# Decode attention over a 65,536-key cache: K turned by VectorE in 32x32 blocks of 32-bit words, a whole chunk's scores in one PSUM bank, four buffers in place of five

## The chip, the cores and the metric

The kernel runs on one core of a Trainium2 chip. The metric is device time in microseconds (us) of one execution. The kernel before takes 1289.4 us (median of 3 runs, 1289.29 to 1289.5). The span in a profile is about 1.7 us shorter than the device time of the same execution. Engines: PE is TensorE's matmul, PEld its weight load, DVE is VectorE, ACT is ScalarE, POOL is GpSimd, SP issues the large loads. "DMA share" is the mean busy share of the core's 16 DMA engines; the "granted clock" is the share of full speed at which PE was allowed to run.

## The reference

One query token, 16 query heads on 8 K/V heads, 65,536 keys of 256 numbers, bfloat16. A small token mixer (branch B) and a gate are mixed in. Cut to what matters:

```python
Hq, Hkv, Sk, Dh = 16, 8, 65536, 256              # x: [1, 1, 448]
q = (x @ wq).reshape(B, Sq, Hq, Dh).transpose(0, 2, 1, 3)
k = jnp.repeat(k_cache, 2, axis=1)               # k_cache, v_cache: [1, 8, 65536, 256]
v = jnp.repeat(v_cache, 2, axis=1)
p = softmax(einsum("bhqd,bhkd->bhqk", q, k) * Dh ** -0.5)
a = einsum("bhqk,bhkd->bhqd", p, v).reshape(B, Sq, Hq * Dh) @ wo
out = g * a + (1 - g) * b                        # b: token mixer, g: gate
```

K and V are 537 MB together and are read once. Everything else is small.

## The kernel before

Each K or V item is a chunk of 8192 keys, 4 MB, in one of five ring buffers. A chunk is worked in four steps of 2048 keys. K comes with keys on the partitions, and this kernel's score matmuls read it with the 256 dimensions there. So PE transposes K (read as 32-bit words, two bfloat16 each) into PSUM, DVE copies that to SBUF, and PE multiplies with the queries in four column strips.

```python
NB = 64; CHUNK = 128 * NB; SB = 16; STEPS = NB // SB; RING = 5; LAG = 4
...
def transposes(n, half):                    # called twice per step
    kn = ring[2 * (n // STEPS) % RING][:].bitcast(FP32).rearrange("p (j k) -> p j k", k=128)
    tp = tps[half]
    j0 = (n % STEPS) * SB + 8 * half
    for jj in range(8):
        nc.tensor.transpose(tp[:, 128 * jj:128 * jj + 128], kn[:, j0 + jj, :], ident[:])
    nc.vector.tensor_copy(
        out=kT[n % 2][:, 8 * DH * half:8 * DH * (half + 1)], in_=tp[:].bitcast(BF16)
    )

def scores(n):
    ...
    for c in range(2):
        for a in range(4):
            nc.tensor.matmul(
                sc[n % 2][32 * a:32 * a + 32, :], lhsT=qT[:, c, g].rearrange("p r x -> p (r x)"),
                rhs=kv[:, :, 32 * a:32 * a + 32, c], start=(c == 0), stop=(c == 1),
                tile_position=(0, 32 * a),
            )
    nc.scalar.activation(out=p_t[n % 2][:], in_=sc[n % 2][:], func=ACT.Exp, scale=scale, accum_out=...)

def p_transpose(n):
    nc.vector.transpose(out=pT_t[n % NPT][:], in_=p_t[n % 2][:])
...
for n in range(n_steps + LAG):
    if n < n_steps:
        transposes(n, 0)
    if 0 <= n - 1 < n_steps:
        scores(n - 1)
    if n < n_steps:
        transposes(n, 1)
    if 0 <= n - 1 < n_steps:
        p_transpose(n - 1)
    ...
    m = n - LAG                              # PV runs four steps behind
    ...                                      # p_v(m): 8 matmuls of 512 columns; then the loads
```

The softmax here doesn't subtract the row's maximum and nothing guards it: scores larger than these inputs give would overflow.

## Time and profile before

| | before |
|---|---|
| device time, median | 1289.4 us |
| span of the profile | 1287.6 us |
| busy PE, DVE, ACT | 74%, 62%, 15% |
| DMA share, 40 to 1240 us | 1.00 |
| last K/V packet ends | 1279.9 us |

Busy time by stretches of the kernel before. The columns are the stretch, its length, busy us of PE, PEld, DVE, ACT and POOL, the granted PE clock, the DMA share and GB/s.

```profile
40.00:640.00 600.00, 447.45 (x3912) 278.66 (x3912) 371.22 (x395) 98.09 (x268) 70.10 (x72) 0.84 1.00 430
640.00:1240.00 600.00, 450.89 (x3966) 281.07 (x3963) 371.03 (x391) 83.98 (x245) 2.31 (x3) 0.85 1.00 429
1266.00:1270.00 4.00, 4.00 (x43) 2.70 (x40) 3.82 (x4) 1.32 (x4) 0.00 (x0) 1.00 0.86 351
1270.00:1274.00 4.00, 4.00 (x45) 2.21 (x43) 3.63 (x5) 0.74 (x3) 0.00 (x0) 1.00 0.58 240
1274.00:1278.00 4.00, 3.22 (x39) 1.96 (x40) 3.82 (x5) 0.69 (x2) 0.00 (x0) 1.00 0.52 209
1278.00:1282.00 4.00, 2.75 (x42) 1.02 (x42) 2.04 (x6) 0.69 (x2) 0.00 (x0) 1.00 0.08 28
```

The mid-kernel is DMA-bound. At the end the DMA does not stop at once. From about 1270 us it runs at a share near 0.5 for some 9 us.

Groups of instructions of the kernel before (line, engine, operation, out<-in, shapes, count | busy us, mean ns | idle time before it and what ended it). K is copied from PSUM four times in this form, 620 us of DVE in all.

```profile
L316 DVE COPY kT_141<-tps_74 128x2048 bf16<-128x2048 bf16 x128 | 154.8, 1209 | 350.5 <-PE tps_74 L315 350.5
L315 PE MATMUL tps_74<-ident,ring_69 128*128 128x128 f32 x416 | 68.7, 318 | 66.6 <-DMA ring_69<-in_A_k_cache_dram 66.5
L325 PE MATMUL sc_77<-kT_142,qT 128*32 128x512 bf16 x1024 | 105.0, 495 | 1.2 <-DVE kT_142 L316 1.2
```

The end of the kernel before, from the timeline (start us, duration us, engine and line, operation, out<-in, count, [idle before <-releaser]):

```profile
1277.92 0.62 PE L325 MATMUL sc_77<-kT_142,qT 128*32 128x512 bf16 x8 [0.78 <-DVE kT_142 L316]
1280.89 0.60 PE L347 MATMUL pv<-ring_71,pT_148 128*4 128x512 bf16 x8
1281.55 0.75 DVE L364 TENSOR_SCALAR pvs<-pv,rden 128x512 f32<-128x512 f32 x1 [0.62 <-PE pv L347]
1285.26 0.32 SPq L432 DMA_DIRECT2D out_dram<-res  x1
```

### The profile page before, as it was taken

What the parts mean: (1) busy time and instruction counts of PE and PEld (TensorE: products, weight loads), DVE (VectorE), ACT (ScalarE), POOL (GpSimd) and SP (SyncE); (2) the same over time, 40 slices, a digit from 0 to 9 for tenths busy, and PEclk for the clock granted to TensorE, in tenths of its full rate; (3) what the DMA queues carried; (4) which work ended last, traced back from release to release, by engine and by line L of the source; (5) the groups of instructions that cost most, each with busy time, mean ns of one, the idle gap of its engine ahead of it and who ended that gap; (6) DMA issues with size and microseconds to landing.
All of it is one profiled execution on the core that took longest, in us unless ns stands there. A gap on an engine that the chain in (4) does not pass through costs nothing.

```text
span 1287.6 us, 19500 instructions
## 1 busy us (share of the span) xinstructions
PE 952.5 (74%) x8454; PEld 595.9 (46%) x8454; DVE 792.6 (62%) x859; ACT 193.2 (15%) x543; POOL 80.2 (6%) x101
## 2 busy tenths in 40 slices
PE   4586777876877767778768677696786876877878
PEld 3354444544544444445445444454454544544544
DVE  3565755756666557566566575674665755656657
ACT  0111111211111111111111111111111111111111
POOL 2110111100111001110000000000000000000000
PEclk9887888888888788788888897887887888889889
DMA  9999999999999999999999999999999999999995
GB/s 392 431 430 433 427 432 425 429 432 429 433 425 433 429 431 428 429 430 429 432 429 426 433 430 430 430 430 427 435 427 433 425 430 431 430 430 418 436 421 241
DMA packets 21196, 545.49 MB, mean 424 GB/s; under 512 B 2675, under 2 KB 2806, under 8 KB 3958
## 3 DMA queue, kind: packets, MB, share of 16 engines
q1 hardware_dynamic: 19730, 540.55, 98.0%
q0 software_dynamic: 1376, 3.69, 0.8%
q8 instruction: 66, 1.08, 0.3%
q14 instruction: 20, 0.16, 0.0%
q10 hardware_dynamic: 4, 0.00, 0.0%
HBM read 544.22 MB, written 0.00 MB: 423 GB/s over the span
## 4 chain that ended last, share of the span: by engine, by line
DMA 62%; PE 37%; DVE 1%; issue 0%; ACT 0%; SPq 0%; ACTq 0%; DVEq 0%
DMA ring_73<-in_A_k_cache_dram 15%; PE tps_74 L315 12%; DMA ring_69<-in_A_k_cache_dram 12%; DMA ring_72<-in_A_k_cache_dram 12%; PE tps_75 L315 12%; DMA ring_71<-in_A_k_cache_dram 12%; DMA ring_70<-in_A_k_cache_dram 11%; PE pv L347 6%; PE sc_77 L325 4%; PE sc_76 L325 3%; DMA ring_73<-in_A_wq_dram 1%; PE misc L292 0%; PE misc L247 0%; DVE kT_142 L316 0%; PE misc L357 0%
## 5 line engine op out<-in xcount | busy, mean ns | idle before, releaser
L316 DVE COPY kT_141<-tps_74 128x2048 bf16<-128x2048 bf16 x128 | 154.8, 1209 | 350.5 <-PE tps_74 L315 350.5
L316 DVE COPY kT_141<-tps_75 128x2048 bf16<-128x2048 bf16 x128 | 156.4, 1222 | 95.2 <-PE tps_75 L315 94.8
L331 ACT ACTIVATE p_144<-sc_77 128x512 bf16<-128x512 f32 x128 | 76.4, 597 | 710.0 <-PE sc_77 L325 710.0
L316 DVE COPY kT_142<-tps_75 128x2048 bf16<-128x2048 bf16 x128 | 156.7, 1224 | 25.2 <-PE tps_75 L315 24.6
L316 DVE COPY kT_142<-tps_74 128x2048 bf16<-128x2048 bf16 x128 | 152.7, 1193 | 7.8 <-PE tps_74 L315 7.3
L331 ACT ACTIVATE p_143<-sc_76 128x512 bf16<-128x512 f32 x128 | 76.4, 597 | 368.8 <-PE sc_76 L325 368.8
L315 PE MATMUL tps_74<-ident,ring_69 128*128 128x128 f32 x416 | 68.7, 318 | 66.6 <-DMA ring_69<-in_A_k_cache_dram 66.5
L315 PE MATMUL tps_74<-ident,ring_71 128*128 128x128 f32 x416 | 68.8, 319 | 65.5 <-DMA ring_71<-in_A_k_cache_dram 65.5
L315 PE MATMUL tps_74<-ident,ring_70 128*128 128x128 f32 x416 | 66.0, 310 | 63.5 <-DMA ring_70<-in_A_k_cache_dram 63.5
L315 PE MATMUL tps_74<-ident,ring_73 128*128 128x128 f32 x416 | 67.0, 313 | 58.5 <-DMA ring_73<-in_A_k_cache_dram 58.0
L315 PE MATMUL tps_74<-ident,ring_72 128*128 128x128 f32 x384 | 62.3, 315 | 63.8 <-DMA ring_72<-in_A_k_cache_dram 63.8
L325 PE MATMUL sc_77<-kT_142,qT 128*32 128x512 bf16 x1024 | 105.0, 495 | 1.2 <-DVE kT_142 L316 1.2
L315 PEld LDWEIGHTS tps_74<-ident,ring_71 128*128 128x128 f32 x416 | 54.6, 163 | 91.5 <-issue 89.4
L315 PEld LDWEIGHTS tps_74<-ident,ring_69 128*128 128x128 f32 x416 | 54.8, 163 | 89.6 <-issue 88.0
L315 PEld LDWEIGHTS tps_74<-ident,ring_70 128*128 128x128 f32 x416 | 52.3, 158 | 86.6 <-issue 84.9
L315 PEld LDWEIGHTS tps_74<-ident,ring_73 128*128 128x128 f32 x416 | 53.1, 160 | 82.4 <-issue 77.6
L315 PEld LDWEIGHTS tps_74<-ident,ring_72 128*128 128x128 f32 x384 | 49.3, 161 | 85.3 <-issue 83.6
L325 PE MATMUL sc_76<-kT_141,qT 128*32 128x512 bf16 x1024 | 79.3, 385 | 0.2
L315 PE MATMUL tps_75<-ident,ring_69 128*128 128x128 f32 x416 | 67.8, 316 | 0.0
L315 PE MATMUL tps_75<-ident,ring_71 128*128 128x128 f32 x416 | 66.7, 312 | 0.0
L315 PEld LDWEIGHTS tps_75<-ident,ring_69 128*128 128x128 f32 x416 | 53.8, 161 | 26.9 <-issue 26.9
L315 PEld LDWEIGHTS tps_75<-ident,ring_71 128*128 128x128 f32 x416 | 52.8, 159 | 27.6 <-issue 27.6
(133 smaller groups left out, 976.5 us busy)
## 6 DMA issues: line engine op xcount, KB each, us to landing
ring_69<-in_A_k_cache_dram SPq DMA_DIRECT2D x13, 4096.0 KB, 25.1
ring_70<-in_A_v_cache_dram SPq DMA_DIRECT2D x13, 4096.0 KB, 34.5
ring_71<-in_A_k_cache_dram SPq DMA_DIRECT2D x13, 4096.0 KB, 24.8
ring_72<-in_A_v_cache_dram SPq DMA_DIRECT2D x13, 4096.0 KB, 34.2
ring_73<-in_A_k_cache_dram SPq DMA_DIRECT2D x13, 4096.0 KB, 24.5
ring_69<-in_A_v_cache_dram SPq DMA_DIRECT2D x13, 4096.0 KB, 33.9
ring_70<-in_A_k_cache_dram SPq DMA_DIRECT2D x12, 4096.0 KB, 24.2
ring_71<-in_A_v_cache_dram SPq DMA_DIRECT2D x12, 4096.0 KB, 33.6
```

What stands on the lines that cost most here:

```text
L315: nc.tensor.transpose(tp[:, 128 * jj:128 * jj + 128], kn[:, j0 + jj, :], ident[:])
L316: nc.vector.tensor_copy(out=kT[n % 2][:, 8 * DH * half:8 * DH * (half + 1)], in_=tp[:].bitcast(BF16))
L325: nc.tensor.matmul(sc[n % 2][32 * a:32 * a + 32, :], lhsT=qT[:, c, g].rearrange("p r x -> p (r x)"), rhs=kv[:, :, 32 * a:32 * a + 32, c], ...
L331: nc.scalar.activation(out=p_t[n % 2][:], in_=sc[n % 2][:], func=ACT.Exp, scale=scale, accum_out=den[g % 2][:, n % steps_g:n % steps_g + 1],)
L347: nc.tensor.matmul(pv[32 * a:32 * a + 4, :], lhsT=pT[:, i, :, 0], rhs=vt[:, j * DH:(j + 2) * DH], start=first and i < 4, stop=last and i > ...
```

## The change

The intent: take K's transposition off PE and the copy out of PSUM off DVE. DVE turns 32x32 blocks of 32-bit words straight from the ring to `kT`. That does not gather a key's 256 dimensions on the partitions. As the kernel's layout takes it, partition 32a+x then holds word x of a 32-word block for the keys that sat on partitions 32a to 32a+31. So the queries are laid out block-diagonally over all 128 rows, and 8 full matmuls per step accumulate over the blocks. The queries' window is shifted by one column per step, so the four steps of a chunk fill different rows of one PSUM bank, and exponential and its transposition run once per chunk. PV of a chunk follows its softmax, so V is released earlier and the ring has four buffers. Cut to its core:

```diff
-RING = 5
-LAG = 4
+SIZES = (4,) * 8
+RING = 4
 ...
-    tps = [psum.tile([128, 8 * 128], FP32, name=f"tps{i}") for i in range(2)]
 ...                                  # pv doubled; queries laid out block-diagonally in qw
-    def transposes(n, half):
-        ...                          # 8 PE transposes into tps[half], one PSUM copy
+    def turn(i, s, n):
+        kn = ring[2 * i % RING][:].bitcast(FP32)
+        nc.vector.transpose(
+            out=kT[n % 2][:].bitcast(FP32), in_=kn[:, s * SB * 128:(s + 1) * SB * 128]
+        )
+    def scores(i, s, n):
+        g, c = divmod(i, n_chunks)
+        kv = kT[n % 2][:].rearrange("p (j b y two) -> p j b y two", j=SB, b=4, two=2)
+        for q in range(8):
+            nc.tensor.matmul(
+                sc[i % 2][:], lhsT=qw[:, g, q, PAD - s:PAD - s + 128], rhs=kv[:, :, q // 2, :, q % 2],
+                start=(s == 0 and q == 0), stop=(s == sizes[c] - 1 and q == 7),
+            )
 ...
+    for i in range(total):
+        g, c = divmod(i, n_chunks)
+        for s in range(sizes[c]):
+            turn(i, s, n)
+            scores(i, s, n)
+            ...
+        if 2 * i + RING < 2 * total:
+            load(2 * i + RING)
+        softmax(i)
+        ...
+        for s in range(sizes[c]):
+            ...p_v(i, s)
+        if 2 * i + 1 + RING < 2 * total:
+            load(2 * i + 1 + RING)
```

More of the change, by code (lines that the diff above doesn't have):

```diff
@@ L17 @@
 DH = 256
-NB = 64
-CHUNK = 128 * NB
 SB = 16
-STEPS = NB // SB
-RING = 5
-LAG = 4
-NPT = LAG + 2
+SIZES = (4,) * 8
+RING = 4
+MAXS = max(SIZES)
+PAD = MAXS - 1
+WIN = 128 + PAD
 GELU_C0 = 0.7978845608028654
@@ L58 @@
     DR = D - DA
-    assert DR == 64 and F % 128 == 0 and SK % CHUNK == 0
-    n_chunks = SK // CHUNK
-    steps_g = n_chunks * STEPS
-    n_steps = HKV * steps_g
-    assert steps_g >= LAG + 4
+    assert DR == 64 and F % 128 == 0 and SK % (128 * SB * sum(SIZES)) == 0
+    sizes = SIZES * (SK // (128 * SB * sum(SIZES)))
+    n_chunks = len(sizes)
+    n_steps = HKV * sum(sizes)
     scale = 1.0 / (DH ** 0.5)
@@ L71 @@
     psum = ctx.enter_context(tc.tile_pool(name="psum", bufs=1, space=bass.MemoryType.PSUM))
-    ring = [ringp.tile([128, NB * DH], BF16, name=f"ring{i}") for i in range(RING)]
-    tps = [psum.tile([128, 8 * 128], FP32, name=f"tps{i}") for i in range(2)]
+    ring = [ringp.tile([128, MAXS * SB * DH], BF16, name=f"ring{i}") for i in range(RING)]
     sc = [psum.tile([128, 512], FP32, name=f"sc{i}") for i in range(2)]
-    pv = psum.tile([128, 512], FP32, name="pv")
+    pv = [psum.tile([128, 512], FP32, name=f"pv{i}") for i in range(2)]
     misc = psum.tile([128, 512], FP32, name="misc")
@@ L85, in piece @@
         g, c = divmod(i, n_chunks)
-        src = (A_v_cache if is_v else A_k_cache)[0, g, c * CHUNK:(c + 1) * CHUNK, :]
-        src = src.rearrange("(p j) d -> p (j d)", j=NB)
+        nb = sizes[c] * SB
+        lo = sum(sizes[:c]) * SB * 128
+        src = (A_v_cache if is_v else A_k_cache)[0, g, lo:lo + 128 * nb, :]
+        src = src.rearrange("(p j) d -> p (j d)", j=nb)
         nc.sync.dma_start(
@@ L92, in load @@
     def load(item):
+        last = sizes[-1]
         if item < 2 * total - 2:
-            piece(item, 0, NB)
+            piece(item, 0, sizes[item // 2 % n_chunks] * SB)
         elif item == 2 * total - 1:
-            k, v = item - 1, item
-            tail = SB // 2 - 2
-            for it, j, n in (
-                (k, 0, SB), (k, SB, SB), (k, 2 * SB, SB), (v, 0, SB), (k, 3 * SB, SB),
-                (v, SB, SB), (v, 2 * SB, SB), (v, 3 * SB, SB - tail), (v, NB - tail, tail),
-            ):
-                piece(it, j, n)
+            for s in range(last - 1):
+                piece(item - 1, s * SB, SB)
+            piece(item, 0, SB)
+            piece(item - 1, (last - 1) * SB, SB)
+            for s in range(1, last - 1):
+                piece(item, s * SB, SB)
+            tail = SB // 2 - 2
+            piece(item, (last - 1) * SB, SB - tail)
+            piece(item, last * SB - tail, tail)
     wq_slot = ring[RING - 1]
@@ L137, in load_wo @@
         )
-    ident = const.tile([128, 128], FP32)
+    ident = const.tile([128, 128], BF16)
     make_identity(nc, ident[:])
@@ L148 @@
     nc.gpsimd.memset(pick[:], 0.0)
-    for t, w, step in ((sel, 4, -1), (pick, 2, -16)):
-        for a in range(4):
-            nc.gpsimd.affine_select(
-                out=t[:], in_=t[:], compare_op=ALU.not_equal, fill=1.0, base=-32 * a,
-                pattern=[[step, w]], channel_multiplier=1,
-            )
+    rows = [(sel, 4, -1, 32 * a) for a in range(4)]
+    rows += [(pick, 2, -16, 32 * a + s) for a in range(4) for s in range(MAXS)]
+    for t, w, step, row in rows:
+        nc.gpsimd.affine_select(
+            out=t[:], in_=t[:], compare_op=ALU.not_equal, fill=1.0, base=-row,
+            pattern=[[step, w]], channel_multiplier=1,
+        )
+    block = const.tile([128, 4], FP32)
+    nc.gpsimd.memset(block[:], 0.0)
+    for a in range(4):
+        nc.gpsimd.memset(block[32 * a:32 * a + 32, a:a + 1], 1.0)
     nc.gpsimd.tensor_copy(
@@ L159 @@
     nc.gpsimd.memset(mhalf[:], -0.5)
-    one_b = const.tile([1, 128], BF16)
-    nc.vector.memset(one_b[:], 1.0)
+    pairs = const.tile([128, 2, 256], BF16)
+    nc.vector.memset(pairs[:, 0, :], 0.0)
+    nc.vector.memset(pairs[:, 0, 0:256:2], 1.0)
+    nc.vector.transpose(out=pairs[:, 1, :].bitcast(FP32), in_=pairs[:, 0, :].bitcast(FP32))
+    one_b = pairs[0:1, 1, 0:256:2]
     one_f = const.tile([1, 128], FP32)
@@ L166 @@
     p_t = [work.tile([128, 512], BF16, name=f"p{i}") for i in range(2)]
-    pT_t = [work.tile([128, 512], BF16, name=f"pT{i}") for i in range(NPT)]
-    den = [work.tile([128, steps_g], FP32, name=f"den{i}") for i in range(2)]
+    pT_t = [work.tile([128, 512], BF16, name=f"pT{i}") for i in range(2)]
+    den = [work.tile([128, n_chunks], FP32, name=f"den{i}") for i in range(2)]
     dsum = work.tile([128, 1], FP32, name="dsum")
@@ L175 @@
     res = work.tile([1, D], BF16, name="res")
-    qT = const.tile([128, 2, HKV, 2, 16], BF16)
+    qT = const.tile([128, 2, HQ], BF16)
+    qw = const.tile([128, HKV, 8, WIN], BF16)
     gate = const.tile([128, 2], FP32)
-    nc.vector.memset(qT[:], 0.0)
-    nc.vector.memset(pv[:], 0.0)
+    nc.vector.memset(qw[:], 0.0)
+    for t in pv:
+        nc.vector.memset(t[:], 0.0)
     nc.vector.memset(acc[:], 0.0)
@@ L215 @@
     xb_ps = sc[0][:, 0:D]
-    nc.tensor.matmul(xb_ps, lhsT=one_b[:], rhs=x_row[:], start=True, stop=True)
+    nc.tensor.matmul(xb_ps, lhsT=one_b, rhs=x_row[:], start=True, stop=True)
     stats = const.tile([128, nc.vector.BN_STATS_DIM], FP32)
@@ L253 @@
             )
-    for c in range(2):
-        nc.vector.tensor_copy(
-            out=qT[:, c, :, :, 0],
-            in_=q_ps[:, c * HQ:(c + 1) * HQ].rearrange("p (g r) -> p g r", r=2),
-        )
+    nc.vector.tensor_copy(out=qT[:].rearrange("p c h -> p (c h)"), in_=q_ps)
+    qr_ps = misc[:, 0:8 * HQ]
+    for b in range(4):
+        for a in range(4):
+            nc.tensor.matmul(
+                qr_ps[32 * a:32 * a + 32, b * 2 * HQ:(b + 1) * 2 * HQ],
+                lhsT=ident[:, 32 * b:32 * b + 32], rhs=qT[:].rearrange("p c h -> p (c h)"),
+                start=True, stop=True, tile_position=(0, 32 * a),
+            )
+    for g in range(HKV):
+        for r in range(2):
+            h = 2 * g + r
+            cols = slice(PAD + 16 * r, PAD + 16 * r + 97, 32)
+            nc.vector.tensor_tensor(
+                out=qw[:, g, :, cols],
+                in0=qr_ps.rearrange("p (b h) -> p b h", h=HQ)[:, :, h:h + 1].to_broadcast([128, 8, 4]),
+                in1=block[:].rearrange("p (o a) -> p o a", o=1).to_broadcast([128, 8, 4]),
+                op=ALU.mult,
+            )
     load(RING - 1)
@@ L265 @@
     gel = work.tile([128, D], BF16, name="gel")
-    MIX = min(8, (n_steps - LAG) // (NF + 1))
+    MIX = min(8, (n_steps - 4) // (NF + 1))
     def mixer(n):
-        b, ph = divmod(n - LAG, MIX)
+        b, ph = divmod(n - 4, MIX)
         if not 0 <= b < NF:
@@ L307, in mixer @@
             )
-    def transposes(n, half):
-        kn = ring[2 * (n // STEPS) % RING][:].bitcast(FP32).rearrange("p (j k) -> p j k", k=128)
-        tp = tps[half]
-        j0 = (n % STEPS) * SB + 8 * half
-        for jj in range(8):
-            nc.tensor.transpose(tp[:, 128 * jj:128 * jj + 128], kn[:, j0 + jj, :], ident[:])
-        nc.vector.tensor_copy(
-            out=kT[n % 2][:, 8 * DH * half:8 * DH * (half + 1)], in_=tp[:].bitcast(BF16)
-        )
-    def scores(n):
-        g = n // steps_g
-        kv = kT[n % 2][:].rearrange("p (j k two) -> p j k two", j=SB, two=2)
-        for c in range(2):
-            for a in range(4):
-                nc.tensor.matmul(
-                    sc[n % 2][32 * a:32 * a + 32, :],
-                    lhsT=qT[:, c, g].rearrange("p r x -> p (r x)"),
-                    rhs=kv[:, :, 32 * a:32 * a + 32, c], start=(c == 0), stop=(c == 1),
-                    tile_position=(0, 32 * a),
-                )
+    def turn(i, s, n):
+        kn = ring[2 * i % RING][:].bitcast(FP32)
+        nc.vector.transpose(
+            out=kT[n % 2][:].bitcast(FP32), in_=kn[:, s * SB * 128:(s + 1) * SB * 128]
+        )
@@ L331, in scores, with softmax @@
+    def scores(i, s, n):
+        g, c = divmod(i, n_chunks)
+        kv = kT[n % 2][:].rearrange("p (j b y two) -> p j b y two", j=SB, b=4, two=2)
+        for q in range(8):
+            nc.tensor.matmul(
+                sc[i % 2][:], lhsT=qw[:, g, q, PAD - s:PAD - s + 128], rhs=kv[:, :, q // 2, :, q % 2],
+                start=(s == 0 and q == 0), stop=(s == sizes[c] - 1 and q == 7),
+            )
+    def softmax(i):
+        g, c = divmod(i, n_chunks)
         nc.scalar.activation(
-            out=p_t[n % 2][:], in_=sc[n % 2][:], func=ACT.Exp, scale=scale,
@@ L333, in scores @@
-            accum_out=den[g % 2][:, n % steps_g:n % steps_g + 1],
-        )
-    def p_transpose(n):
-        nc.vector.transpose(out=pT_t[n % NPT][:], in_=p_t[n % 2][:])
-    def p_v(n, lo=0, hi=SB // 2):
-        vt = ring[(2 * (n // STEPS) + 1) % RING]
-        pT = pT_t[n % NPT][:].rearrange("p (i b x) -> p i b x", b=4, x=16)
-        first = n % steps_g == 0
-        last = n % steps_g == steps_g - 1
-        for i in range(lo, hi):
-            j = (n % STEPS) * SB + 2 * i
-            a = i % 4
+            out=p_t[i % 2][:], in_=sc[i % 2][:], func=ACT.Exp, scale=scale,
@@ L347, in p_v @@
+            accum_out=den[g % 2][:, c:c + 1],
+        )
+        nc.vector.transpose(out=pT_t[i % 2][:], in_=p_t[i % 2][:])
+    def p_v(i, s, lo=0, hi=SB // 2):
+        g, c = divmod(i, n_chunks)
+        vt = ring[(2 * i + 1) % RING]
+        pT = pT_t[i % 2][:].rearrange("p (i b x) -> p i b x", b=4, x=16)
+        first = c == 0 and s == 0
+        last = c == n_chunks - 1 and s == sizes[c] - 1
+        for k in range(lo, hi):
+            j = s * SB + 2 * k
+            a = k % 4
             nc.tensor.matmul(
-                pv[32 * a:32 * a + 4, :], lhsT=pT[:, i, :, 0], rhs=vt[:, j * DH:(j + 2) * DH],
@@ L349, in p_v @@
-                start=first and i < 4, stop=last and i >= SB // 2 - 4, tile_position=(0, 32 * a),
+                pv[g % 2][32 * a:32 * a + 4, :], lhsT=pT[:, k, :, s], rhs=vt[:, j * DH:(j + 2) * DH],
+                start=first and k < 4, stop=last and k >= SB // 2 - 4, tile_position=(0, 32 * a),
             )
@@ L364, in o_scale @@
         nc.vector.tensor_scalar(
-            out=pvs[:], in0=pv[:], scalar1=rden[:, 0:1], scalar2=None, op0=ALU.mult
+            out=pvs[:], in0=pv[g % 2][:], scalar1=rden[:, 0:1], scalar2=None, op0=ALU.mult
         )
@@ L390, in o_out @@
             load_wo(g + 2)
-    def epilogue(n):
-        m = n - LAG
-        if m < 0:
-            return
-        g, s = divmod(m, steps_g)
-        if s == 0 and g > 0:
-            o_turn(g - 1)
-        if s == 1 and g > 0:
-            o_out(g - 1)
-        if s == steps_g - 3:
+    n = 0
+    for i in range(total):
+        g, c = divmod(i, n_chunks)
+        for s in range(sizes[c]):
+            turn(i, s, n)
+            scores(i, s, n)
+            mixer(n)
+            if c == 0 and g > 0:
+                if s == 0:
+                    o_turn(g - 1)
+                if s == 1:
+                    o_out(g - 1)
+            n += 1
+        if 2 * i + RING < 2 * total:
+            load(2 * i + RING)
+        softmax(i)
+        if c == n_chunks - 1:
             den_sum(g)
-        if s == steps_g - 2:
             den_tot(g)
-    for n in range(n_steps + LAG):
-        if n < n_steps:
-            transposes(n, 0)
-        if 0 <= n - 1 < n_steps:
-            scores(n - 1)
-        if n < n_steps:
-            transposes(n, 1)
-        if 0 <= n - 1 < n_steps:
-            p_transpose(n - 1)
-        mixer(n)
-        epilogue(n)
-        m = n - LAG
-        if m >= 0:
-            if m == n_steps - 1:
-                p_v(m, 0, SB // 4 + 1)
-                p_v(m, SB // 4 + 1)
-            else:
-                p_v(m)
-            if m % steps_g == steps_g - 1:
-                o_scale(m // steps_g)
-        for k, item in ((m, 2 * (m // STEPS) + 1 + RING), (n, 2 * (n // STEPS) + RING)):
-            if 0 <= k < n_steps and k % STEPS == STEPS - 1 and item < 2 * total:
-                load(item)
+        for s in range(sizes[c]):
+            if i == total - 1 and s == sizes[c] - 1:
+                p_v(i, s, 0, SB // 4 + 1)
+                p_v(i, s, SB // 4 + 1)
+            else:
+                p_v(i, s)
+        if 2 * i + 1 + RING < 2 * total:
+            load(2 * i + 1 + RING)
+        if c == n_chunks - 1:
+            o_scale(g)
     o_turn(HKV - 1)
```

## The prediction

> **What bounds the kernel now.** DMA. The page's strip shows DMA at 9 tenths or more in every slice but the last; the kernel must read 544.2 MB. Busy time by stretches shows a DMA share of 1.00 and 429 to 430 GB/s from 40 to 640 us and from 640 to 1240 us. The engines have room: PE 74%, DVE 62%. The chain of waits gives DMA 62%, PE 37%, but that PE share is work on a chunk after its K landed: the list of waits shows the first transposes of each chunk waiting for K on all five buffers (58 to 67 us each). [...]
>
> Only the ends are not DMA time. Start: the first K lands at 23 us, behind wq, with the queue full meanwhile. End: the timeline shows PE without pause from 1250 to 1277 us, 3.13 us per step, and DMA falling to about 235 GB/s at 1269 us and to nothing at 1279.5. The last PV ends at 1281.5; scale, turn, output and store take 6 us to 1287.6.
>
> **What changes, per step of 2048 keys (256 steps; K and V are 2.1 MB, 4.88 us at 430 GB/s).**
> - Removed: 16 fp32 PE transposes (about 2.1 us of PE) and two PSUM copies on DVE of 1.2 us each (620 us in all).
> - Added: one DVE 32x32 transpose of 2048 words. The existing one takes 701 ns for 512 elements; a one-column VectorE operation takes about 0.17 us, which leaves 1.04 ns per element: estimate 2.3 us. [...]
> - Scores: 8 matmuls in four column strips (0.62 us) become 8 full ones, estimated 1.7 to 2.2 us at full clock.
> - Exponential and its transposition: once in four steps (ACT about 193 to 75 us).
> - PV: the same 0.6 us, but after the whole chunk's scores.
>
> Per step DVE goes from 3.1 to 2.5 us, PE from 3.13 to about 2.5: both below 4.88. A chunk's chain of turns, last scores, exponential, transposition and PV takes about 4 x 2.3 + 1.9 + 0.6 + 0.7 + 2.5 = 15 us after K lands, under the 19.5 us of DMA per chunk. V slots come free earlier than before (then four steps behind), so four buffers keep at least two 4 MB items queued.
>
> **On the critical path:** almost nothing. Bytes, descriptor sizes and order stay. The PE backlog at the end goes, so the finish follows the last V piece directly: 1 to 2 us gained. The longer set-up (a 4.4 us memset, 16 products for the queries) hides before the first K lands.
>
> **Predicted: 1287 us, 8 in 10 between 1280 and 1294.** Faster by over 2%: 2%; within 2%: 93%; slower by over 2%: 5%.
>
> **Signs.** Right: DMA share 1.00 and about 430 GB/s in the same two stretches; the turn 2.2 to 2.4 us, DVE busy near 650 us; PE busy 550 to 750 us; turns waiting on DMA of K; the last PV waiting for the last V piece. Wrong: DMA share below 0.97 in mid-kernel, with loads waiting for a slot.
>
> **What would make it wrong.** [...] If the DMA rate depends on what engines do to SBUF, the whole time shifts, either way. A low PE clock in short bursts would lengthen scores to 3.4 us, still just hidden.

The forecast's sum is the 1289.4 us of the kernel before less the 1 to 2 us at the end, put at 1287 us. The turn's 2.3 us is an estimate from the kernel before, 0.17 us (a one-column reciprocal, L360 at 1280.57 us) and 2048 words at 1.04 ns (701 ns for 512 elements, L337, less 0.17 us). For the scores' 1.7 to 2.2 us, as a check, four matmuls of 448 columns took 0.92 us at full clock there (L383, 1283.67 us), which is 2.1 us for eight of 512. The 3.4 us is twice 1.7; the records of the granted clock of the kernel before hold 62 stretches at 0.50 and 62 at 1.00. As an estimate from the 1.04 ns, a turn of twice the time per word would take 4.4 us, four of them with the rest of the chain about 21 us, more than a chunk's 19.5 us of DMA, and DVE would bind.

## More of the kernel before

Lines of the profile page of the kernel before: the span, busy time by engine, the strip of 40 slices for DMA (tenths of busy share), and the DMA queues with packets, megabytes and share.

```profile
span 1287.6 us, 19500 instructions
PE 952.5 (74%) x8454; PEld 595.9 (46%) x8454; DVE 792.6 (62%) x859; ACT 193.2 (15%) x543; POOL 80.2 (6%) x101
DMA  9999999999999999999999999999999999999995
DMA packets 21196, 545.49 MB, mean 424 GB/s; under 512 B 2675, under 2 KB 2806, under 8 KB 3958
q1 hardware_dynamic: 19730, 540.55, 98.0%
q8 instruction: 66, 1.08, 0.3%
q14 instruction: 20, 0.16, 0.0%
```

DMA is full in every slice but the last.

In the packet records about 16 packets are in flight up to 1268 us and about 9 from 1270 to 1275: about half of the 16 DMA engines have finished, and the other half have not.

## The result, and the profile after

The changed kernel takes 1282.64 us (median of 4, 1282.46 to 1283.01), the kernel before in the same rounds 1289.35 us (1289.15 to 1289.5). The ratio is 0.9948 (95% interval 0.9931 to 0.9966). Ratios here are the mean time of one kernel's fast runs over that of the other's of the same rounds, so not quite the ratio of the medians quoted. The gain of 6.7 us is inside the forecast range and within 2%, but more than three times the 1 to 2 us that the prediction's sum held.

The same lines of the profile page, of the changed kernel:

```profile
span 1280.9 us, 10091 instructions
PE 754.8 (59%) x4374; PEld 287.3 (22%) x4374; DVE 661.4 (52%) x429; ACT 62.6 (5%) x159; POOL 82.9 (6%) x118
DMA  9999999999999999999999999999999999999996
DMA packets 21154, 544.88 MB, mean 425 GB/s; under 512 B 2675, under 2 KB 2806, under 8 KB 3958
q1 hardware_dynamic: 19730, 540.55, 98.4%
q8 instruction: 34, 0.56, 0.2%
q14 instruction: 10, 0.08, 0.0%
```

The load queue q1 is the same to the packet. What fell is the number of instructions, 19,500 to 10,091, and with it the two instruction queues: 66 packets to 34, and 20 to 10.

Busy time by stretches of the changed kernel:

```profile
40.00:640.00 600.00, 351.43 (x1982) 131.91 (x1982) 309.54 (x186) 36.53 (x86) 67.80 (x70) 0.86 1.00 430
640.00:1240.00 600.00, 364.53 (x2035) 137.22 (x2033) 304.29 (x177) 21.31 (x62) 2.31 (x3) 0.84 1.00 430
1262.00:1266.00 4.00, 3.43 (x16) 1.36 (x15) 3.15 (x2) 0.00 (x0) 0.00 (x0) 1.00 1.00 415
1266.00:1270.00 4.00, 1.95 (x10) 0.77 (x8) 2.31 (x1) 0.00 (x0) 0.00 (x0) 1.00 0.62 252
1270.00:1274.00 4.00, 2.43 (x27) 1.08 (x29) 1.08 (x4) 0.69 (x2) 0.00 (x0) 1.00 0.33 135
```

The half-share stretch at the end is shorter, and the last K/V packet ends at 1273.9 us in place of 1279.9. That is 6.0 of the 6.7 us. The rest is the stretch behind it: 7.7 us before (1279.9 to 1287.6), 7.0 us after (1273.9 to 1280.9).

Groups of the changed kernel that answer to those above, and the end of its timeline:

```profile
L343 DVE STREAM_TRANSPOSE kT_182<-ring_69 128x2048 f32<-128x2048 f32 x64 | 147.6, 2306 | 171.1 <-DMA ring_69<-in_A_k_cache_dram 151.2
L351 PE MATMUL sc_73<-kT_182,qw 128*128 128x512 bf16 x512 | 188.9, 533 | 246.0 <-DVE kT_182 L343 246.0
```

```profile
1266.78 2.31 DVE L343 STREAM_TRANSPOSE kT_183<-ring_71 128x2048 f32<-128x2048 f32 x1 [1.64 <-DMA ring_71<-in_A_k_cache_dram]
1269.15 1.90 PE L351 MATMUL sc_74<-kT_183,qw 128*128 128x512 bf16 x8 [2.05 <-DVE kT_183 L343]
1272.92 1.90 PE L373 MATMUL pv_76<-ring_72,pT_187 128*4 128x512 bf16 x32
1274.88 0.75 DVE L390 TENSOR_SCALAR pvs<-pv_76,rden 128x512 f32<-128x512 f32 x1 [1.49 <-PE pv_76 L373]
1278.59 0.32 SPq L449 DMA_DIRECT2D out_dram<-res  x1
```

The turn takes 2.3 us as estimated, and waits for K's DMA. The last PV was predicted to wait for the last V piece. It does not: it starts at 1272.92 without a DMA wait, behind the chain from the last K piece (turn, scores, exponential, transposition).

**Theory A.** Instructions come by DMA too, on the same 16 engines. The profile's queue q8, which it calls "instruction", moved 66 packets of 16 KB, 1.08 MB, in the kernel before, where PE has 8454 matmuls and as many weight loads, 16,908. In the changed kernel it moved 34 packets, 0.56 MB, for 8748. That is 64 bytes for each of PE's instructions in both, so q8 is taken to be PE's; such a packet is called a fetch here. In the packet records one such fetch holds a DMA engine for 1.07 us, and while it runs there are 16 packets in flight with it counted, so it takes an engine from the loads. Between 60 and 1240 us, 58 of the 61 fetches of the kernel before (29 of 31 in the changed one) have a K/V packet that began as the fetch ended and took 1.67 to 1.77 us, typically 1.71, where 1.21 is normal. So a fetch costs about 1.57 us of one engine, an estimate: 1.07 and the 0.5 more of the packet behind it. If fetches fell evenly on 16 engines, 32 fewer would give 3.1 us; if they fall on eight, 6.3 us. The measured 6.0 us and the half-share at the end point to eight.

**Theory B.** The PE backlog at the end is gone, as predicted, and is worth more than thought.

**Theory C.** The ring of four, the earlier release of V and the one softmax per chunk change when loads are issued, and so bring the DMA engines' ends closer together.

### The profile page after: what moved, and what is told of

It is laid out like the page before. It is cut to its first block, busy times and chain, and to the rows that moved or that the text cites. A ratio compares the mean times of both kernels' runs of the same rounds, so it can differ in the third digit from the quotient of the medians.

```text
span 1280.9 us, 10091 instructions
## 1 busy us (share of the span) xinstructions
PE 754.8 (59%) x4374; PEld 287.3 (22%) x4374; DVE 661.4 (52%) x429; ACT 62.6 (5%) x159; POOL 82.9 (6%) x118
## 4 chain that ended last, share of the span: by engine, by line
DMA 64%; DVE 17%; PE 16%; issue 2%; DVEq 0%; SPq 0%; ACT 0%; ACTq 0%
DMA ring_69<-in_A_k_cache_dram 58%; PE sc_73 L351 13%; DVE kT_182 L343 9%; DVE kT_183 L343 7%; DMA ring_71<-in_A_k_cache_dram 6%; PE sc_74 L351 1%; DVE acc L334 1%; PE misc L399 1%; PE misc L409 1%; PE misc L322 0%; DVE acc L414 0%; PE pv_76 L373 0%; DVE pT_187 L362 0%; DVE oT L403 0%; DVEq L343 0%
## 5 line engine op out<-in xcount | busy, mean ns | idle before, releaser
L351 PEld LDWEIGHTS <-qw 128*128 128x128 bf16 x2048 | 222.2, 111 | 779.7 <-issue 322.5
L351 PE MATMUL sc_73<-kT_182,qw 128*128 128x512 bf16 x512 | 188.9, 533 | 246.0 <-DVE kT_182 L343 246.0
L343 DVE STREAM_TRANSPOSE kT_182<-ring_69 128x2048 f32<-128x2048 f32 x64 | 147.6, 2306 | 171.1 <-DMA ring_69<-in_A_k_cache_dram 151.2
L351 PE MATMUL sc_74<-kT_182,qw 128*128 128x512 bf16 x512 | 147.5, 437 | 118.5 <-DVE kT_182 L343 118.0
L343 DVE STREAM_TRANSPOSE kT_182<-ring_71 128x2048 f32<-128x2048 f32 x64 | 147.0, 2296 | 120.2 <-DMA ring_71<-in_A_k_cache_dram 93.9
L351 PE MATMUL sc_73<-kT_183,qw 128*128 128x512 bf16 x512 | 148.3, 439 | 25.1 <-DVE kT_183 L343 25.1
L343 DVE STREAM_TRANSPOSE kT_183<-ring_71 128x2048 f32<-128x2048 f32 x64 | 145.7, 2277 | 3.4 <-DMA ring_71<-in_A_k_cache_dram 1.6
L343 DVE STREAM_TRANSPOSE kT_183<-ring_69 128x2048 f32<-128x2048 f32 x64 | 145.5, 2273 | 2.5 <-PE sc_73 L351 2.5
L351 PE MATMUL sc_74<-kT_183,qw 128*128 128x512 bf16 x512 | 130.7, 398 | 17.7 <-DVE kT_183 L343 17.7
L362 DVE STREAM_TRANSPOSE pT_186<-p_184 128x512 bf16<-128x512 bf16 x32 | 22.8, 711 | 100.9 <-ACT p_184 L358 100.9
L362 DVE STREAM_TRANSPOSE pT_187<-p_185 128x512 bf16<-128x512 bf16 x32 | 22.8, 711 | 86.7 <-ACT p_185 L358 86.7
L358 ACT ACTIVATE p_184<-sc_73 128x512 bf16<-128x512 f32 x32 | 19.1, 597 | 714.9 <-PE sc_73 L351 714.9
L373 PE MATMUL pv_75<-ring_70,pT_186 128*4 128x512 bf16 x512 | 30.4, 379 | 24.4 <-DVE pT_186 L362 24.4
L373 PE MATMUL pv_76<-ring_70,pT_186 128*4 128x512 bf16 x512 | 30.4, 379 | 24.4 <-DVE pT_186 L362 24.4
L373 PEld LDWEIGHTS <-pT_186 128*4 128x4 bf16 x1024 | 22.1, 87 | 87.3 <-DVE pT_186 L362 64.6
L358 ACT ACTIVATE p_185<-sc_74 128x512 bf16<-128x512 f32 x32 | 19.1, 597 | 454.0 <-PE sc_74 L351 454.0
L373 PE MATMUL pv_75<-ring_72,pT_187 128*4 128x512 bf16 x512 | 30.4, 379 | 18.3 <-DVE pT_187 L362 18.3
L373 PE MATMUL pv_76<-ring_72,pT_187 128*4 128x512 bf16 x512 | 30.4, 379 | 18.3 <-DVE pT_187 L362 18.3
L373 PEld LDWEIGHTS <-pT_187 128*4 128x4 bf16 x1024 | 22.1, 86 | 71.3 <-DVE pT_187 L362 48.4
L334 DVE SCALAR_TENSOR_TENSOR acc<-misc,half_g,acc 1x448 f32<-1x448 f32 x14 | 9.4, 671 | 53.1 <-PE misc L322 53.1
L311 POOL TENSOR_SCALAR t_b<-t_b 128x448 f32<-128x448 f32 x14 | 7.9, 564 | 357.7 <-ACT t_b L303 357.7
L136 POOL DMA_DIRECT2D wo_96<-in_A_wo_dram x4 | 3.1, 784 | 301.7 <-PE misc L409 301.7
```

The source lines that it names most:

```text
L136: nc.gpsimd.dma_start(out=wo_t[g % 2][:], in_=A_wo[g * 512:(g + 1) * 512, :].rearrange("(q p) n -> p q n", p=128),)
L311: nc.gpsimd.tensor_scalar(out=t_b[:], in0=t_b[:], scalar1=GELU_C1, scalar2=1.0, op0=ALU.mult, op1=ALU.add)
L334: nc.vector.scalar_tensor_tensor(out=acc[:], in0=misc[0:1, 0:D], scalar=half_g[0:1, 0:1], in1=acc[:], op0=ALU.mult, op1=ALU.add,)
L343: nc.vector.transpose(out=kT[n % 2][:].bitcast(FP32), in_=kn[:, s * SB * 128:(s + 1) * SB * 128])
L351: nc.tensor.matmul(sc[i % 2][:], lhsT=qw[:, g, q, PAD - s:PAD - s + 128], rhs=kv[:, :, q // 2, :, q % 2], start=(s == 0 and q == 0), stop= ...
L358: nc.scalar.activation(out=p_t[i % 2][:], in_=sc[i % 2][:], func=ACT.Exp, scale=scale, accum_out=den[g % 2][:, c:c + 1],)
```

## The experiments

On the chips of the later calls, fast runs of one kernel often fall into two groups about 2 us apart (the changed kernel: 1282.59 and 1282.83 beside 1285.07 to 1285.11; the kernel before: 1288.69 to 1289.18 beside 1290.86 to 1291.32). The traces show where the 2 us lie. In those of the lower group (the changed kernel, the kernel before, after_again, wide8, pad128, pvhalf2, poolpad64) 6.9 to 7.7 us pass from the last K/V packet to the end. In those of longer runs (kfirst 1284.4, before_dveturn 1284.34, before_dveturn_pad 1289.99, pad64 1291.16) it is 8.4 to 9.7 us, and PE's granted clock is 0.50 in part or all of that stretch while PE still works: kfirst's last twelve matmuls took 3.5 us at 0.50 where the changed kernel's took 2.0 at full clock. No run of the changed kernel's upper group was profiled, and why the clock is low just then is not known. The end of the last K/V packet in the trace lies before that stretch, and it is the cleaner measure; it is used beside the medians and the ratios to the kernel before of the same rounds. For unchanged loads and count it repeats within 0.3 us (1273.9 in the changed kernel, 1274.2 in after_again).

### Adding PE instructions to the changed kernel: pad64 and pad128

```diff
             else:
                 p_v(i, s)
+        if i < total - 1:
+            for _ in range(64):              # 128 in pad128
+                nc.tensor.matmul(
+                    pad[0:1, 0:1], lhsT=ident[:, 0:1], rhs=ident[:, 0:1], start=True, stop=True
+                )
```

(`pad` is a new PSUM bank that nothing reads.)

> The changed kernel plus 64 one-column matmuls into an unused PSUM bank behind the PV of every chunk but the last: 8064 more PE instructions (weight load and matmul each), which brings PE back to about the instruction count of the kernel before (16,908), with about 2 us of PE time per chunk put where PE waits for the next K anyway. Theory A (the gain is fewer instruction fetches: 66 packets of 16 KB fell to 34, each holding one DMA engine 1.07 us and lengthening the next K/V packet there by 0.5 us, and landing on the engines that finish last): 31 more fetches x 1.57 us = 49 us of engine time, so +5 to +6.5 us if it falls on the slower half of the engines, 1288 to 1289 us; +3 us if it is spread over all 16. Theory B (the gain is the PE backlog at the end that went): no change, 1282.6. Theory C (ring of four, earlier release of V): no change, 1282.6.

> As pad64 with 128 of the small matmuls per chunk: 16,128 more PE instructions, 63 more fetches. Theory A: twice the step of pad64, +10 to +13 us (1293 to 1295.5) if on half the engines, +6 if on all 16, provided the chunk chain (15 us plus about 4) stays under 19.5 us. Theories B and C: 1282.6, or a little more only if PE becomes tight, which would show as K slots being reloaded late and a DMA share below 1.

Measured: pad64 1289.29 us (1288.51 to 1291.16), ratio 0.9996 (0.998 to 1.0013). pad128 1295.20 us (1294.72 to 1296.10), ratio 1.0045 (1.003 to 1.006). The kernel before took 1289.59 us in these rounds. So 8064 idle instructions take back the whole gain, and twice as many put the changed kernel 5.6 us behind the kernel before. In the profile of pad64, and then in the busy time by stretches of pad128:

```profile
q8 instruction: 65, 1.06, 0.3%
```

```profile
1272.00:1276.00 4.00, 4.00 (x120) 3.32 (x116) 2.09 (x1) 0.00 (x0) 0.00 (x0) 1.00 0.82 330
1276.00:1280.00 4.00, 3.34 (x17) 1.40 (x15) 3.29 (x2) 0.00 (x0) 0.00 (x0) 1.00 0.50 211
1280.00:1284.00 4.00, 2.87 (x13) 1.01 (x11) 1.29 (x2) 0.69 (x2) 0.00 (x0) 1.00 0.49 197
```

The share at the end stands at 0.50 and 0.49, for about 10 us: eight engines late, eight done, if those at work are full. The last K/V packet ends at 1279.7 us in pad64 and 1285.6 in pad128. Of theory A's two forms, the one with eight engines is right (+5.8 and +11.7 us on 1273.9, expected +5 to +6.5 and +10 to +13). B and C expected no change. The count alone is enough to make a difference of this size; that nothing else made it is left to before_dveturn_pad below.

### Control, PE work without instructions: wide8

```diff
+        if i < total - 1:
+            for _ in range(8):
+                nc.tensor.matmul(
+                    pad[:], lhsT=ident[:], rhs=qw[:, 0].rearrange("p q w -> p (q w)")[:, 0:512],
+                    start=True, stop=True,
+                )
```

> Control for PE activity: instead of 64 small matmuls, 8 matmuls of 512 columns per chunk (1.7 to 3.4 us of PE per chunk, at least as much PE work as pad64 adds[...]) but only 1008 more instructions, 4 more fetches. Theory A: +0.3 to +0.9 us, 1283 to 1283.5. If PE activity or reads of SBUF by PE slow the DMA: as much as pad64 or more.

Measured: 1283.22 us (1282.99 to 1283.48), ratio 0.9951; q8 had 38 packets, as its page says:

```profile
PE 845.6 (66%) x4815; PEld 329.3 (26%) x4878; DVE 661.6 (52%) x429; ACT 62.7 (5%) x159; POOL 82.9 (6%) x118
q8 instruction: 38, 0.62, 0.2%
```

The last K/V packet ended at 1274.3 us. PE was busy 845.6 us, close to pad64's 852.3 and far above the changed kernel's 754.8. Over 63 chunks that is 1.4 us more per chunk in wide8 and 1.5 in pad64, where the expectations had 1.7 to 3.4 and about 2. So it is not PE's activity that costs, but the number of its instructions.

### One part of the change alone, in the kernel before: before_dveturn and before_dveturn_pad

```diff
     def transposes(n, half):
         kn = ...
-        tp = tps[half]
         j0 = (n % STEPS) * SB + 8 * half
-        for jj in range(8):
-            nc.tensor.transpose(tp[:, 128 * jj:128 * jj + 128], kn[:, j0 + jj, :], ident[:])
-        nc.vector.tensor_copy(
-            out=kT[n % 2][:, 8 * DH * half:8 * DH * (half + 1)], in_=tp[:].bitcast(BF16)
+        nc.vector.transpose(
+            out=kT[n % 2][:, 8 * DH * half:8 * DH * (half + 1)].bitcast(FP32),
+            in_=kn[:, j0:j0 + 8, :].rearrange("p j k -> p (j k)"),
         )
```

before_dveturn_pad adds 16 of the one-column matmuls to every step but the last four.

> The kernel before with one part of the change alone: K turned by VectorE as 32-bit words in two halves per step, no PE transposes and no PSUM copies; five buffers, softmax per step and PV four steps behind stay. The queries are not rearranged, so the result is wrong on purpose. It has 8192 PE instructions fewer than before, as the changed kernel has. Theory A: nearly the whole gain, 1282 to 1283.5. Theory B: also the whole gain, since the PE backlog goes with the transposes. Theory C (ring, release of V, one softmax per chunk): stays within 2 us of the kernel before, 1287 to 1289.

> The kernel before with K turned by VectorE (result not the reference's, as before_dveturn) plus 16 one-column matmuls per step, 8064 PE instructions, so that PE has as many instructions as the kernel before but none of its transposes and PSUM copies. Instruction theory: 1283.2 + 6 = 1289, the time of the kernel before, with 66 fetches. If transposes on PE or the PSUM copies were themselves what slowed the DMA: 1283.2.

Measured: before_dveturn 1283.21 us (1282.70 to 1284.34), ratio 0.9952, q8 34 packets, last K/V packet at 1273.7 us. before_dveturn_pad 1289.67 us (1288.64 to 1290.08), ratio 0.9995, q8 65 packets, last K/V packet at 1279.6 us. Both score with the wrong pairs of words on purpose. The comparison with the reference passed them all the same (and pvhalf2 below, which leaves out half of PV), so on these inputs it does not catch wrong scores, and that the changed kernel passes it does not prove its scores right. From the page of before_dveturn, and then from the page of before_dveturn_pad and its busy time by stretches:

```profile
q8 instruction: 34, 0.56, 0.2%
```

```profile
q8 instruction: 65, 1.06, 0.3%
1270.00:1275.00 5.00, 1.90 (x16) 0.42 (x16) 3.01 (x5) 0.69 (x2) 0.00 (x0) 0.50 0.54 226
1275.00:1280.00 5.00, 4.17 (x39) 1.29 (x40) 1.72 (x6) 0.69 (x2) 0.00 (x0) 0.74 0.33 133
```

The turn on DVE alone gives nearly the whole gain, with five buffers and one softmax per step, so theory C is not needed. With the transposes and PSUM copies gone but the instructions back, the gain is gone too. So neither the transposes nor the copies slowed the DMA, nor was PE's backlog what cost: it is the count. PE's granted clock was lower in these two (0.575 and 0.553 as a mean, 0.856 in the changed kernel), and the last K/V packet ended where the count says all the same. Nor is the gain from the fewer instructions of the other engines: q14 still had 17 packets in before_dveturn, where the changed kernel has 10.

These kernels also bear out the eight. In the packet records the early engines of before_dveturn_pad end near 1266.5 us, as in the changed kernel; only the late ones moved, from about 1272 to 1274 us to about 1278 to 1279.6. With four buffers the early engines are held back too (near 1271 us in pad64, 1274.5 in pad128): in these two kernels the 16 engines stood idle 1.6 and 3.0 us each on average between 60 and 1240 us, in before_dveturn_pad 0.0.

### The ring part alone, in the kernel before: before_ring4

```diff
-RING = 5
+RING = 4
```

> The kernel before with four buffers in place of five: the ring part of the change alone. Instruction theory: the count is the same, so the same 66 fetches and the same time as before, 1289 to 1290. If the shorter queue of loads were what brought the DMA engines' ends together, 1283 to 1287.

Measured: 1304.11 us (1301.41 to 1307.24), ratio 1.0109 (1.0091 to 1.0127). Neither expectation: it loses about 14 us. Busy time by stretches of this kernel, to set beside 430 and 429 GB/s with five buffers:

```profile
40.00:640.00 600.00, 446.31 (x3896) 277.21 (x3896) 370.79 (x394) 98.10 (x268) 70.12 (x72) 0.84 1.00 425
640.00:1240.00 600.00, 445.59 (x3896) 278.04 (x3896) 365.08 (x384) 82.52 (x240) 2.31 (x3) 0.84 0.99 422
```

By the packet records the DMA engines stood idle 7.5 us each on average between 60 and 1240 us (0.3 in the kernel before, 0.0 in the changed one), and a 32 KB packet took 1232 ns on average in place of 1221. With PV four steps behind, V holds its buffer too long for four. The changed kernel can afford four because PV follows its own chunk. That part of the change gains no time; it pays for the buffer that was taken away. Why packets were slower too stays open; it is not all of them (the median was 1213 ns, and 1215 in the kernel before), but a few per cent that took much longer.

### The end of the kernel: kfirst

The last chunk's four K pieces are issued before any of its V pieces; in the changed kernel the fourth K piece is behind the first V piece.

```diff
-            for s in range(last - 1):
-                piece(item - 1, s * SB, SB)
-            piece(item, 0, SB)
-            piece(item - 1, (last - 1) * SB, SB)
-            for s in range(1, last - 1):
+            for s in range(last):
+                piece(item - 1, s * SB, SB)
+            for s in range(last - 1):
                 piece(item, s * SB, SB)
```

> The changed kernel with the last chunk's pieces in another order: all four K pieces, then the V pieces (before: the fourth K piece behind the first V piece). In the profile of the changed kernel the last PV did not wait for the last V piece, as predicted, but for the transposed probabilities: last K piece landed at 1266.8, PV began at 1272.9, DMA had nothing left at about 1273.9. If the end is bound by the chain behind the last K piece, this piece lands up to 2.4 us earlier, the PV of the first three steps runs before the last V piece lands, and the time falls by 0.5 to 1 us, to about 1282 where the changed kernel gives 1282.6. If the end is bound by the last V piece, no change.

Measured: 1284.20 us (1282.90 to 1284.45), ratio 0.9950, no gain. From the timeline of kfirst:

```profile
1273.76 0.59 PE L371 MATMUL pv<-ring,pT 128*4 128x512 bf16 x5 [0.81 <-DMA ring<-in_A_v_cache_dram]
1274.67 0.39 PE L371 MATMUL pv<-ring,pT 128*4 128x512 bf16 x3 [0.32 <-DMA ring<-in_A_v_cache_dram]
1275.91 1.87 PE L397 MATMUL misc<-sel,pvs 128*128 128x2 f32 x8 [0.85 <-DVE pvs L388]
```

PV now waits for V's last pieces, and ends at 1275.06 us where the changed kernel's ended at 1274.82. So the two chains, from the last K piece and from the last V piece, end within a fraction of a microsecond of each other, and shortening one shows the other. The next eight matmuls took 1.87 us where the changed kernel took 1.05, at a granted clock of 0.50: this trace is of the upper group. The two runs of the lower one, 1282.90 and 1283.06 us, are those to set beside the changed kernel's 1282.46 to 1283.01: no gain there either.

### Another engine's instructions: poolpad and poolpad64

```diff
+        if total // 2 <= i < total - 1:
+            for _ in range(256):             # 64 in poolpad64
+                nc.gpsimd.memset(ppad[:], 0.0)
```

> The changed kernel with 256 one-column GpSimd memsets behind each of the chunks 32 to 62: 7936 more instructions on GpSimd, none on PE. If any engine's instruction fetch costs DMA time as PE's does: 31 more fetches, +3 (all engines) to +6 us (half of them), 1285.5 to 1289. If GpSimd's instructions come by another way or are not fetched by these DMA engines: 1282.6 and no more packets in the instruction queues.

> The GpSimd padding again, a quarter of it, so that GpSimd keeps up (64 one-column memsets, about 10 us of GpSimd, behind each of the chunks 32 to 62): 1984 more GpSimd instructions, 15 to 16 more fetches of 8 KB. In the trace of the first padding one DMA engine alone ended 12 us behind the others after 31 more such fetches. If a GpSimd stream is fetched by one DMA engine: +4 to +6 us, 1286.5 to 1288.5, with a single engine ending late, for a quarter of the instructions of the kernel with 64 small matmuls. If spread: +1 us or less.

poolpad measured 1914.00 us: GpSimd could not keep up and was still setting its column 600 us after the loads, so its time says nothing of fetches. Its packet records do: 15 of the engines' last packets ended between about 1273 and 1276 us, and one at 1285.7 us. poolpad64, where GpSimd keeps up: 1286.28 us (1286.08 to 1286.55), ratio 0.9970 where the changed kernel on the same chip had 0.9953. q14 had 26 packets of 8 KB in place of 10, and the last K/V packet ended at 1277.0 us, 3.1 us later. The direction is right and the step somewhat under the 4 to 6 us expected. So GpSimd's 1984 instructions cost half of what 8064 cost on PE: fewer and smaller fetches, but the late end of a single packet chain says that they all fall on one DMA engine. That it is one engine is read from the ends; the records do not number the engines. An estimate from the packet records fits it. Such a fetch holds its engine for 0.31 us, and the K/V packet behind it takes 1.57 us in place of 1.21, so 0.66 us in all. Sixteen of them on one of the engines that end early in the changed kernel, near 1266.5 us, give 1277.1 us, and 1277.0 was measured. So the first 7 us of this cost would be hidden behind the late engines, which is why the step is small.

### Moving other load between engines: wo_eight

```diff
     def load_wo(g):
+        if g < 3:
+            for lo in range(0, 128, 8):
+                nc.gpsimd.dma_start(out=wo_t[g % 2][lo:lo + 8], in_=...[lo:lo + 8])
+            return
```

> The changed kernel with the wo loads of the first three groups issued as 16 DMAs of 8 partitions each in place of one of 128 (1.4 MB in all). A test of what sets the time: in all traces so far about half of the 16 DMA engines end 6 to 10 us before the rest. If a DMA of 8 rows is carried by 8 fixed engines, these carry 1.38 MB, 0.17 MB or 6.5 us each, and the other eight are relieved of 0.086 MB, 3.2 us each. If the eight are those that end early, the time falls by 2 to 3 us (1280); if they are those that end late, it rises by about 3 us (1285.5); if the rows go round all engines, no change beyond 0.5 us.

Measured: 1300.56 us (1299.53 to 1302.31), ratio 1.0082. The 48 small loads stalled GpSimd, the mixer's steps on it came late, PE and ACT waited (ACT up to 50 us at once), and the loads got 399 GB/s from 40 to 240 us, 430 GB/s again from 640 us. Waiting is only part of it: the DMA share in that stretch was 0.98, and a 32 KB packet took 1286 ns on average where the changed kernel has 1219. The test is spoiled by this and decides nothing. The gap between the two halves' ends was 5.5 us, as in the changed kernel, so these loads are not seen to have shifted one half against the other. Whether the late half can be relieved stays open.

### Below the changed kernel's count: after_again, pvhalf and pvhalf2

```diff
-        for k in range(lo, hi):
+        for k in range(lo, hi if i == total - 1 else 4):
```

> The changed kernel unedited, on the same chip as the three others of this call, to compare them with: 1282.6 us as before, with 34 instruction fetches in the PE stream.

> The changed kernel with half of the PV matmuls left out in all chunks but the last (result wrong on purpose): 2016 PE instructions fewer, weight loads and matmuls, 8 fetches of 16 KB fewer (26 in place of 34). Instruction theory, by the slope of the two padded kernels (6 us for 31.5 fetches): -1.5 us, 1281.1. If the time below 34 fetches is bound by something else: 1282.6.

> As pvhalf, mended (the accumulation groups of the first seven groups are closed): the changed kernel with half of the PV matmuls left out in all chunks but the last (result wrong on purpose), 2016 PE instructions fewer, 26 fetches of 16 KB in place of 34. Instruction theory, by the slope of the padded kernels: -1.5 us against the changed kernel, so 1281.1 (ratio to before about 0.9935 where the changed kernel has 0.9948 to 0.9953), and the last K/V packet at 1272.4 us of the trace where the changed kernel had 1273.9. If the time below 34 fetches is bound by something else: no change.

pvhalf was refused by the check before the chip, because an accumulation group was left open; pvhalf2 closes it.

after_again: 1285.07 us (1282.59 to 1285.11, the two groups told of above), ratio 0.9953, last K/V packet at 1274.2 us. pvhalf2: 1281.83 us (1281.66 to 1282.35), ratio 0.9939, q8 26 packets, last K/V packet at 1272.6 us, 1.3 us before the changed kernel's and 1.6 before after_again's. Expected were 1.5 us. So at the last K/V packet the slope holds below 34 fetches as well. In the medians it is 0.8 us, and the ratio says little: the interval, 0.9925 to 0.9952, holds the changed kernel's 0.9948 too, and all five runs of pvhalf2 are of the lower group while its kernel before has both.

### All of it in one table

| kernel | PE instructions | 16 KB fetches | last K/V packet, us | median, us | ratio |
|---|---|---|---|---|---|
| pvhalf2 | 6,732 | 26 | 1272.6 | 1281.83 | 0.9939 |
| changed | 8,748 | 34 | 1273.9 | 1282.64 | 0.9948 |
| before_dveturn | 8,716 | 34 | 1273.7 | 1283.21 | 0.9952 |
| wide8 | 9,756 | 38 | 1274.3 | 1283.22 | 0.9951 |
| before_dveturn_pad | 16,780 | 65 | 1279.6 | 1289.67 | 0.9995 |
| pad64 | 16,812 | 65 | 1279.7 | 1289.29 | 0.9996 |
| before | 16,908 | 66 | 1279.9 | 1289.35 | 1 |
| pad128 | 24,876 | 97 | 1285.6 | 1295.20 | 1.0045 |

(PE instructions are weight loads and matmuls, twice the page's count of weight loads. The last K/V packet is from one trace of each kernel.) From 34 to 97 fetches the end moves by 11.7 us, 0.186 us per fetch. One fetch's 1.57 us shared by eight engines is 0.196 us. Two quite different kernel structures lie on the same line.

No kernel here computes the right result faster than the changed one. The only run below it, pvhalf2, leaves work out.

## Why the prediction was right or wrong

- **DMA bounds the kernel, and it stays so.** Right: share 1.00 and 430 GB/s in both stretches after the change. The total, 1287 us with a range of 1280 to 1294, held the 1282.64 us measured, and "within 2%" was right.
- **"Bytes, descriptor sizes and order stay ... almost nothing" on the critical path.** This is the step that failed in size. It is true of the loads (q1 is the same to the packet) and not of the DMA engines' work. Instruction fetches fell from 66 to 34 packets. The expected gain from that term was 0; it measured 6.0 us at the end of the last K/V packet, and 32 x 0.186 = 5.95 us by the padded kernels' slope. The page showed the term before the change: 19,500 instructions and 1.08 MB in the queue called instruction. A share of 0.3% was read as an average over 16 engines, and the ends say that it is not spread over 16: 0.186 us per fetch were measured, where 1.57 us spread over 16 would be 0.098.
- **"The PE backlog at the end goes, so the finish follows the last V piece directly: 1 to 2 us gained."** The backlog went, but the stretch behind the last K/V packet shrank by only 0.7 us (7.7 to 7.0), and PV did not wait for the last V piece. It waited for the chain behind the last K piece; kfirst shows that both chains end almost together.
- **The DVE turn at 2.3 us per step.** Right: 2.27 to 2.31 us. The size of the element made no difference: with the 0.17 us that the prediction took as the fixed part, 2048 words of 32 bits took 1.03 to 1.04 ns each, and the 512 bfloat16 elements before (701 ns) 1.04 ns each.
- **Scores 1.7 to 2.2 us per step at full clock, PE busy 550 to 750 us.** 1.90 us at full clock, and 3.4 to 3.6 us at a granted clock of 0.50 to 0.53 in the first steps of the three chunks that were looked at (637.6, 657.0 and 1247.0 us); PE was busy 754.8 us, just above the range. DVE 661 us (650 expected), ACT 62.6 us (75 expected).
- **Four buffers are enough.** Right for the changed kernel: no DMA engine stood idle between 60 and 1240 us. before_ring4 shows that it rests on the early release of V, as the prediction had argued.
- **The set-up hides.** Right: the first turn starts at 23.3 us, as the first transpose did before. But the memset of the queries was put at 4.4 us, and the trace has 7.04 us for its 8384 bfloat16 elements (L192), 0.84 ns each, after 1.7 us with no recorded work. 4.4 us was an estimate that fits 4192 words of 32 bits at 1.04 ns each, and this memset is not recorded as words of 32 bits. Others are: the 256 bfloat16 elements of L199 appear as 128 of uint32, in 0.17 us.

What stays open: which DMA engines fetch PE's instructions and whether the eight are fixed (the records carry no engine number), why PE's clock is low at the end of some runs, and the slower packets of before_ring4.

## What to carry to other kernels

In this kernel, bound by DMA (share 1.00), instructions were loads too: each 16 KB fetch moved the end of the last load by 0.186 us. So count the instructions of each engine, look at the packets of the instruction queues, and ask how many DMA engines share them: here the late half set the end of the loads, with about 9 packets in flight after the rest had ended, and the mean share of 0.3% did not show it. The share near 0.5 in the last microseconds did: the engines ended apart, and its length (some 9 us before) says how far. When a change that should be neutral gains or loses a fraction of a per cent, add idle instructions until the old count is back; here that test cost one run. And look at the end of the last load in the trace, not at the time alone: here the stretch behind it varied by 2 us with PE's granted clock.
